# Moving left products behind the last head outputs, one exponential earlier, and a new order of one segment in four

## The chip, the cores and the metric

The kernel runs on one core of one Trainium2 chip. The metric is the device time of a whole execution in microseconds (us), from the slowest core, which here is the only one. Five engines take part: PE (TensorE, the matrix products), DVE (VectorE), ACT (ScalarE), POOL (GpSimd) and SP (SyncE, which here issues nearly all transfers). Each engine works through its own instructions in the order in which they were written, and waits on semaphores for the others. Sums of products stand in PSUM, eight banks of 2 KB for each of 128 partitions; all else that is in use stands in SBUF, and the program calls it the arena.

## The reference, cut to what matters

A recurrent attention with memory tokens (A), a gated feed-forward network (B), and a mix of both by a gate per row.

```python
for s in range(64):                                # 2048 positions, 32 to a segment
    h = concatenate([mem, x[:, 32*s:32*s+32]])     # 8 memory rows and 32 positions, 640 wide
    q, k, v = h @ Wq, h @ Wk, h @ Wv               # 32 heads of 192
    p = softmax(where(mask, (q @ k.T) * scale, -1e9))
    o = (p @ v) @ Wo                               # summed over the heads
    mem = o[:, :8]; outs.append(o[:, 8:])
a = concatenate(outs)
b = (gelu(x @ w_gate) * (x @ w_up)) @ w_down       # 640 -> 1536 -> 640
out = g * a + (1 - g) * b                          # g = sigmoid((x * gate_w).sum(-1))
```

The memory rows of a segment come out of the segment before it, so that the 64 segments are worked one after the other, and each ends with a chain on which the next one waits.

## The kernel before, in words

The feed-forward part comes first (the first 180 us or so) and leaves its result in DRAM. The rest of the time are the 64 segments, 22 to 24 us each.

**Octets, groups and steps.** The 32 heads of a segment are four octets of eight heads, which the text numbers in the order of work: first to fourth octet, `i` = 0 to 3 in the code (odd segments take them in reverse order, so that the weights loaded last are used first). Queries, keys and values of the octets are made in six groups (`GROUPS`, L523): Q and K of the first octet; V of the first with Q and K of the second; V of the second with Q and K of the third; V of the third with Q of the fourth; K of the fourth; V of the fourth. A group is accumulated in five projection steps, each over 128 of the 640 input columns, an item `("g", n, k)` for step `k` of group `n` (`proj`, L1110). A step of one product is four matmuls side by side, in the four column strips of TensorE (L1132; where the stationary operand is kept from the product before, L226). After the fifth step ScalarE copies the result out of PSUM (queries and keys L1153, values L1156).

**One octet behind its projections.** Each of these is an item in the list of the segment:

- `("tq", i)`, `("tk", i)`: VectorE transposes the rows of queries and keys (L1170); GpSimd copies a part of the queries (L1173).
- `("sc", i)`: scores (`scores`, L1177): the mask as a product (L1181), then the products of queries and keys (L1189, L234, L1196); VectorE takes the maximum (L1208) and subtracts it (L1210).
- `("ex", i)`: softmax (L1213): the exponential on ScalarE (L1220), the sum (L1222), its reciprocal (L1224) and the division (L1226, L1227) on VectorE.
- `("pt", i)`: the probabilities are transposed on TensorE (L1243, L1248) and copied out by ScalarE (L1261; for the fourth octet L1255, with VectorE at L1257).
- `("pv", i)`: head outputs, values times probabilities (`pv_oct`, L1264; products L1276 and L1278), copied out by ScalarE (L1308, for the fourth octet L1298) and VectorE (L1302).
- `("wo", i, h)`: output products, half `h` of octet `i`: two products by two slices ("pairs") of the output weights. L1326 for the first three octets, L1352 for the last four pairs; at place 3 (below) L1370.

The head outputs ask for a free bank of PSUM (`misc_bank`, L1100), as each group does at its first step: the bank that has been free for longest.

**Places.** A place is the number of a segment modulo four. Of the 40 rows of a segment, 32 go through the projections of the segment itself: the 8 memory rows and 24 positions. The queries, keys and values of its last 8 positions don't depend on the segment before, and those of four segments, 32 rows, are made together ahead of time: these are the *left products* (`left_mm`, L911; product L924, and L226 with the kept operand). The item `("lf", place, u, k)` is step `k` (0 to 4) of unit `u`, two product steps (queries and keys) for the next group of four segments; `("le", place, u, m)` copies them out (L1397 on). All places but place 3 walk the same list, but an `lf` or `le` item is executed only in segments of its place, and only where there is a later group of segments (15 of the 16 segments of each place). Place 0 has one unit, place 1 two, place 2 one. At place 3 the list is another: the output products are made for its own rows and for the left rows of the whole group together (`wo_both`, L1366), and `("vb", k)` are left products of values. `PROGS` (L546) names the list of each place, and `segment` (L1449) walks it. The order of the work on every engine is the order of these lists, written out by hand; semaphores follow from what each operation reads and writes.

**Weights.** The weights of the attention don't fit into SBUF. In each segment 13 pieces of the query, key and value weights (384 KB each) and 3 of the output weights (480 KB) are loaded again, in place of a piece just used: after each item, `swap_loads` (L644) issues on SP the transfer of the piece that comes into the slot of one that the item has used up (`load_piece`, L627), and the transfer waits for the last product that reads the old piece. What is loaded is needed late in the same segment: by the fourth octet's projections and the last output products.

**The end of a segment.** The last output products (L1352) are added up with the earlier ones by VectorE (L1567) and transposed (L1570); the first projection steps of the next segment that use the memory rows wait for that.

The stretch of the list around the change, for places 0 to 2 (L524 on):

```python
("ex", 2), ("lf", 2, 1, 2), ("pv", 1), ("wo", 0, 0), ("g", 4, 0), ...
("g", 5, 0), ("g", 5, 1), ("lf", 1, 1, 2), ("lf", 0, 1, 1), ("pt", 2), ("wo", 0, 1), ("tk", 3), ("sc", 3),
("pv", 2), ("g", 5, 2), ("wo", 1, 0), ("ex", 3), ("g", 5, 3), ("wo", 1, 1), ("g", 5, 4), ("wo", 2, 0),
("pt", 3), ("lf", 0, 1, 2), ("wo", 2, 1), ("pv", 3), ("wo", 3, 0), ("wo", 3, 1), ...
```

and the walk over it:

```python
for n, item in enumerate(PROGS[q]):
    ...
    elif kind == "lf":
        if i == q and unit(s, item[2]):
            ...
            left_mm(*unit(s, item[2]), item[3], unit_piece)
    ...
    swap_loads(s, item)
```

Of the kernel before, what the change touches and what calls it, by code (L numbers as in the profile page):

```python
# [238 lines left out]
def _build(nc, A_x, A_mem0, A_Wq, A_Wk, A_Wv, A_Wo, seg_len, w_gate, w_up, w_down,  # L239
# [278 lines left out]
    def piece_view(key, o):  # L518
        if key[0] == 3:
# [4 lines left out]
    PROG = [("g", 0, 0), ("g", 0, 1), ("g", 0, 2), ("g", 0, 3), ("g", 0, 4), ("tq", 0), ("g", 1, 0), ("g", 1, 1),  # L524
# [12 lines left out]
    PROG3 = [("g", 0, 0), ("g", 0, 1), ("g", 0, 2), ("g", 0, 3), ("g", 0, 4), ("g", 1, 0), ("tq", 0), ("tk", 0),  # L537
# [8 lines left out]
    PROGS = (PROG, PROG, PROG, PROG3)  # L546
    assert NOCT == 4
    WOP = 4
    NWP = NT
# [14 lines left out]
    def seg_order(s):  # L564
        keys = []
        for item in PROGS[s % 4]:
            if item[0] == "g":
# [810 lines left out]
    mids, n_wos, to_store = set(), [], []  # L1378
    for x, prog in enumerate(PROGS):
        at = prog.index  # L1380
# [5 lines left out]
        for u in range(2):  # L1386
# [6 lines left out]
            else:  # L1393
                assert at(("le", x, u, 0)) > max(at(("wo", 3, 1)), at(("pv", 3)))
    nqkvs = [[i for i, item in enumerate(prog) if item[0] == "g"][-1] for prog in PROGS]

# [36 lines left out]

    assert all(prog.index(("wo", NOCT - 2, 1)) < prog.index(("pv", NOCT - 1)) for prog in PROGS[:3])
    assert all(prog.index(("sc", NOCT - 1)) < prog.index(("pv", NOCT - 2)) and ("g", 3, EK) in prog[:prog.index(("sc", NOCT - 1))] for prog in PROGS)
    ek_at = [prog.index(("pv", NOCT - 2)) for prog in PROGS]

# [176 lines left out]
def bass_gated_mix__memory_aug_recurrent_mem_tr__glu_gated_geglu__prompt_kernel(  # L1614
    nc,
    A_x,
    A_mem0,
    A_Wq,
    A_Wk,
    A_Wv,  # L1620
    A_Wo,
    A_seg_len,
    B_x,
    B_w_gate,
    B_w_up,
    B_w_down,
    gate_w,
    out,
):
    _build(nc, A_x, A_mem0, A_Wq, A_Wk, A_Wv, A_Wo, A_seg_len, B_w_gate, B_w_up, B_w_down, gate_w, out)  # L1630
# [33 lines left out]
```

## Time and profile before

| | before |
|---|---|
| three runs | 1675.04, 1670.88, 1674.64 us |
| their median | 1674.64 us |
| the profiled execution | 1667.93 us |
| its span, first to last instruction | 1666.2 us |
| PE, products | busy 1567.0 us, 94%, 37090 instructions |
| PEld, weight loads of TensorE (beside PE) | 773.4 us, 46% |
| DVE | 998.3 us, 60% |
| ACT | 783.7 us, 47% |
| POOL | 546.0 us, 33% |
| granted TensorE clock | 0.995 of full speed |
| transfers | 499.28 MB, 300 GB/s on average; the queue of the weights holds the 16 DMA engines for 84.3% of the span |

The profile is one execution, recorded instruction by instruction. Three views of it are used. One gives, for a list of stretches of time, each engine's busy time in the stretch: from left to right the stretch and its length, the busy time and number of instructions of PE, PEld, DVE, ACT and POOL, the granted clock, the busy share of the DMA engines, and GB/s. The second is a time line: start, duration in us, engine, line, operation, destination and source, the tile with its type, and the number of instructions that the row joins; brackets at the end hold the time waited ahead of it and the operation that ended the wait. Several matmuls are in flight together, so that a row of products is counted from its start to the start of the row behind it. The third lists, for one line, what ended its waits: engine and line, us in total, how often. The rows of transfers ("DMA issues") give the engine that issues, how many, KB of each and the median us from issue to landing.

### The profile page before, as it was taken

The numbers are of one execution on the slowest core, as the hardware profiler recorded it, in microseconds if no ns is written. First come the engines' busy times: TensorE is split into PE (matmuls) and PEld (weight loads), VectorE is DVE, ScalarE is ACT, GpSimd is POOL, SyncE is SP. The second block draws the span as 40 slices with busy tenths as digits, with TensorE's granted clock in tenths as the row PEclk, the third lists the DMA queues.
The fourth block names the chain that finished last, engine by engine and source line by source line (L and its number), as shares of the span: only waits on it lengthen the run. The fifth ranks groups of instructions, "written<-read, shape, count | busy, mean of one in ns | idle before, by whom it ended". The sixth has DMA issues, their size and how long they took to land. (4 is left out here: it accounts for less than half of the span.)

```text
span 1666.2 us, 75811 instructions
## 1 busy us (share of the span) xinstructions
PE 1567.0 (94%) x37090; PEld 773.4 (46%) x28147; DVE 998.3 (60%) x3023; ACT 783.7 (47%) x1874; POOL 546.0 (33%) x1609
## 2 busy tenths in 40 slices
PE   9999899999999999999999999999999999999986
PEld 4444345444444445454444444454544444444543
DVE  6453566666566666666665666656665656656653
ACT  2222454545455454545454554545454555545452
POOL 1110233333333333333333333333333333333332
PEclk9999999999999999999999999999999999999998
DMA  9915999989899898989888898989888888988894
GB/s 292 345 47 157 321 319 324 317 315 313 310 323 334 299 323 292 331 317 332 299 310 302 317 343 283 313 290 326 322 296 309 301 326 318 316 292 311 312 326 163
DMA packets 275415, 499.28 MB, mean 300 GB/s; under 512 B 121119, under 2 KB 136327, under 8 KB 275079
## 3 DMA queue, kind: packets, MB, share of 16 engines
q1 hardware_dynamic: 271000, 491.30, 84.3%
q8 instruction: 255, 4.18, 1.0%
q10 hardware_dynamic: 4079, 3.14, 0.6%
q14 instruction: 81, 0.66, 0.1%
HBM read 473.25 MB, written 21.09 MB: 297 GB/s over the span
## 5 line engine op out<-in xcount | busy, mean ns | idle before, releaser
L1132 PE MATMUL ps<-arena 128*32 128x384 bf16 x8640 | 640.3, 329 | 19.6 <-DVE arena L1570 11.4
L226 PE MATMUL ps<-arena 128*32 128x384 bf16 x8960 | 635.9, 327 | 3.5 <-ACT arena L1153 1.2
L1132 PEld LDWEIGHTS ps<-arena 128*32 128x32 bf16 x8640 | 226.8, 96 | 390.8 <-issue 270.0
L1170 DVE STREAM_TRANSPOSE arena<-arena 128x384 bf16<-128x384 bf16 x512 | 273.7, 559 | 71.5 <-ACT arena L1153 70.2
L1153 ACT ACTIVATE arena<-ps 128x384 bf16<-128x384 f32 x512 | 230.3, 493 | 109.7 <-PE ps L1132 102.0
L1173 POOL COPY arena<-arena 64x160 bf16<-64x160 bf16 x256 | 81.3, 318 | 371.0 <-DVE arena L1170 368.9
L1326 PE MATMUL ps<-arena 128*32 128x320 bf16 x3456 | 180.9, 300 | 5.7 <-issue 3.2
L1156 ACT ACTIVATE arena<-ps 128x384 bf16<-128x384 f32 x256 | 124.9, 488 | 112.4 <-PE ps L1132 112.4
L1208 DVE TENSOR_REDUCE arena<-ps 104x4 f32<-104x160 f32 x256 | 83.0, 324 | 149.9 <-PE ps L1196 149.9
L1308 ACT ACTIVATE arena<-ps 128x480 bf16<-128x480 f32 (+1 forms) x208 | 116.6, 561 | 102.7 <-PE ps L1278 99.4
L1261 ACT ACTIVATE arena<-ps 128x448 bf16<-128x448 f32 x192 | 104.6, 545 | 122.8 <-PE ps L1248 122.6
L1006 POOL COPY arena<-arena 128x96 bf16<-128x96 bf16 x256 | 69.4, 271 | 231.1 <-PE ps L1196 159.4
L1222 DVE TENSOR_REDUCE arena<-ps 104x4 f32<-104x160 f32 x256 | 82.5, 322 | 97.6 <-ACT ps L1220 96.7
L1220 ACT ACTIVATE ps<-ps 104x160 f32<-104x160 f32 x256 | 75.7, 296 | 136.8 <-DVE ps L1210 134.9
L1370 PE MATMUL ps<-arena 128*64 128x320 bf16 x1536 | 124.9, 305 | 1.4 <-issue 0.6
L1276 PE MATMUL ps<-arena 128*64 128x160 bf16 x1536 | 119.0, 241 | 3.6 <-issue 3.5
L1326 PEld LDWEIGHTS ps<-arena 128*32 128x32 bf16 x3456 | 90.8, 96 | 47.2 <-ACT arena L1255 11.2
L924 PE MATMUL ps<-arena 128*32 128x384 bf16 x1280 | 108.7, 328 | 0.7 <-issue 0.7
L1278 PE MATMUL ps<-arena 128*64 128x64 bf16 x1536 | 104.3, 193 | 2.4 <-issue 2.1
L1316 POOL COPY arena<-arena 128x96 bf16<-128x96 bf16 x192 | 51.3, 267 | 162.7 <-ACT arena L1298 97.0
L1276 PEld LDWEIGHTS ps<-arena 128*64 128x64 bf16 x1536 | 81.7, 109 | 48.3 <-ACT arena L1156 19.4
L1398 ACT ACTIVATE arena<-ps 128x384 bf16<-128x384 f32 x120 | 57.2, 490 | 92.5 <-DVE arena L1570 41.4
(102 smaller groups left out, 2351.7 us busy)
## 6 DMA issues: line engine op xcount, KB each, us to landing
arena<-in_A_Wk_dram SPq DMA_DIRECT2D x335, 384.0 KB, 6.4
arena<-in_A_Wv_dram SPq DMA_DIRECT2D x335, 384.0 KB, 8.7
arena<-in_A_Wo_dram SPq DMA_DIRECT2D x205, 480.0 KB, 5.9
arena<-in_A_Wq_dram SPq DMA_DIRECT2D x209, 384.0 KB, 5.6
arena<-left_qk_scratch SPq DMA_DIRECT2D x126, 96.0 KB
left_qk_scratch<-arena SPq DMA_DIRECT2D x49, 192.0 KB, 5.2
left_qk_scratch<-arena SPq DMA_DIRECT2D x30, 96.0 KB, 5.5
ffn_b_scratch<-arena ACTq DMA_DIRECT2D x16, 160.0 KB, 4.1
```

The costliest lines, as they stand in the source:

```text
L226: return e.add_instruction(mybir.InstMatmult(name=nm, start_tensor_calc=like["start"], stop_tensor_calc=stop, tile_size=(128, 32), tile_po ...
L924: fns.append(lambda e, outp=outp, rhs=rhs, j=j: e.matmul(outp, lhs, rhs, start=(k == 0), stop=(k == KT - 1), tile_position=(0, 32 * j)))
L1132: fns.append(lambda e, outp=outp, rhs=rhs, j=j: e.matmul(outp, lhs, rhs, start=(k == 0), stop=(k == KT - 1), tile_position=(0, 32 * j)))
L1153: S_.add("act", lambda e, m=m, bk=bk: e.activation(out=rows_sb[m], in_=ps[:, bk, 0:384], func=ACTF.Copy), reads=[r_ps[bk]], writes=[r_rows ...
L1156: S_.add("act", lambda e, i=i, bk=bk: e.activation(out=v_sb[i % NVB].rearrange("p (c n) -> p c n", c=3), in_=ps[:, bk, 0:384].rearrange("p ...
L1170: S_.add("dve", lambda e: e.transpose(out=dst[:, :, 0:L], in_=rows_sb[m].rearrange("p (c r) -> p c r", r=L)), reads=[r_rows[m]], writes=[r ...
L1261: S_.add("act", lambda e: e.activation(out=PT, in_=ps[:, bank, 0:PTW + 128], func=ACTF.Copy), reads=[r_ps[bank]], writes=[r_PT], name="pT ...
L1276: return [lambda e: e.matmul(full, v[:, e0:e0 + 64], PTm[:, i], start=True, stop=False, tile_position=(0, 64 * i), skip_group_check=True), ...
L1278: lambda e: e.matmul(part, vl[:, e0:e0 + 64], PTl[:, i], start=False, stop=True, tile_position=(0, 64 * i), skip_group_check=True)]
L1308: S_.add("act", lambda e: e.activation(out=apx(u[:, 0, 0, :], [[rs, na], [3 * rs, 4], [1, R]]), in_=ps[:, A, 0:na * W].rearrange("p (c t r ...
L1326: fns.append(lambda e, i=i, t=t, j=j, gv=gv: e.matmul(ps[32 * j:32 * j + 32, bank, 0:2 * DJ].rearrange("p (h n) -> p h n", h=2), lhs2[i], ...
L1370: S_.add("pe", [lambda e, i=i, g_=g_, c=c, p=p: e.matmul(ps[64 * i:64 * i + 64, LB, 0:2 * DJ], U3[:, p % 4, c, :], g_[:, c, 2 * DJ * i:2 * ...
```

## The change

Three edits, all to the written-out orders.

1. **Places 0 to 2**, list `PROG`. Item `("lf", 2, 1, 2)`, a left product step of place 2, goes from between `("ex", 2)` and `("pv", 1)` to behind `("pv", 3)`, the fourth octet's head outputs. Items `("lf", 0, 1, 1)`, ahead of `("pt", 2)`, and `("lf", 0, 1, 2)`, between `("pt", 3)` and `("wo", 2, 1)`, both of place 0, go there too. All stand ahead of `("wo", 3, 0)`, the first of the last output products.
2. **Place 1** gets a list of its own, `PROG1`: `PROG` with `("ex", 3)`, the fourth octet's softmax, ahead of `("pv", 2)` instead of two items behind it.
3. **Place 3**, list `PROG3`, is written in another order. The projection steps keep their order among themselves, the output products and the left value products theirs, and so do the loads behind each kind. The fourth octet's key steps `("g", 4, 2)` and `("g", 4, 3)` now stand ahead of the output products `("wo", 0, 0)`, and its last value step `("g", 5, 4)` ahead of `("wo", 2, 0)`; the second scores follow the first step of group 3, with the first head outputs right behind them, which stood three steps later; transpositions and softmaxes move by some places.

The group numbered 4 holds the keys of the fourth octet and group 5 its values. Nothing is added to or taken from the work: each segment executes the same items as before.

```diff
--- before.py
+++ after.py
@@ -526,24 +526,26 @@
             ("g", 2, 2), ("lf", 1, 0, 0), ("pt", 0), ("tq", 1), ("tk", 1), ("sc", 1), ("g", 2, 3), ("g", 2, 4),
             ("tq", 2), ("ex", 1), ("lf", 2, 1, 0), ("lf", 1, 0, 1), ("lf", 1, 0, 2), ("pv", 0), ("g", 3, 0),
             ("tk", 2), ("g", 3, 1), ("g", 3, 2), ("g", 3, 3), ("pt", 1), ("lf", 2, 1, 1), ("g", 3, 4), ("sc", 2),
-            ("ex", 2), ("lf", 2, 1, 2), ("pv", 1), ("wo", 0, 0), ("g", 4, 0), ("g", 4, 1), ("lf", 0, 1, 0),
-            ("g", 4, 2), ("lf", 1, 0, 3), ("lf", 1, 0, 4), ("lf", 1, 1, 0), ("lf", 1, 1, 1), ("le", 1, 0, 0),
-            ("tq", 3), ("g", 4, 3), ("le", 1, 0, 1), ("g", 4, 4), ("g", 5, 0), ("g", 5, 1), ("lf", 1, 1, 2),
-            ("lf", 0, 1, 1), ("pt", 2), ("wo", 0, 1), ("tk", 3), ("sc", 3), ("pv", 2), ("g", 5, 2), ("wo", 1, 0),
-            ("ex", 3), ("g", 5, 3), ("wo", 1, 1), ("g", 5, 4), ("wo", 2, 0), ("pt", 3), ("lf", 0, 1, 2),
-            ("wo", 2, 1), ("pv", 3), ("wo", 3, 0), ("wo", 3, 1), ("lf", 2, 1, 3), ("lf", 2, 1, 4), ("le", 2, 1, 0),
-            ("le", 2, 1, 1), ("lf", 1, 1, 3), ("lf", 1, 1, 4), ("le", 1, 1, 0), ("le", 1, 1, 1), ("lf", 0, 1, 3),
-            ("lf", 0, 1, 4), ("le", 0, 1, 0), ("le", 0, 1, 1)]
-    PROG3 = [("g", 0, 0), ("g", 0, 1), ("g", 0, 2), ("g", 0, 3), ("g", 0, 4), ("g", 1, 0), ("tq", 0), ("tk", 0),
-            ("g", 1, 1), ("g", 1, 2), ("sc", 0), ("g", 1, 3), ("ex", 0), ("g", 1, 4), ("tq", 1), ("g", 2, 0),
-            ("tk", 1), ("g", 2, 1), ("g", 2, 2), ("g", 2, 3), ("g", 2, 4), ("sc", 1), ("tk", 2), ("g", 3, 0),
-            ("pt", 0), ("tq", 2), ("g", 3, 1), ("g", 3, 2), ("g", 3, 3), ("ex", 1), ("pv", 0), ("g", 3, 4),
-            ("sc", 2), ("pt", 1), ("ex", 2), ("g", 4, 0), ("g", 4, 1), ("wo", 0, 0), ("g", 4, 2), ("g", 4, 3),
-            ("g", 4, 4), ("tq", 3), ("tk", 3), ("wo", 0, 1), ("pv", 1), ("sc", 3), ("g", 5, 0), ("pt", 2),
-            ("wo", 1, 0), ("wo", 1, 1), ("ex", 3), ("pv", 2), ("g", 5, 1), ("g", 5, 2), ("g", 5, 3), ("pt", 3),
-            ("wo", 2, 0), ("g", 5, 4), ("wo", 2, 1), ("pv", 3), ("vb", 0), ("vb", 1), ("vb", 2), ("wo", 3, 0),
+            ("ex", 2), ("pv", 1), ("wo", 0, 0), ("g", 4, 0), ("g", 4, 1), ("lf", 0, 1, 0), ("g", 4, 2),
+            ("lf", 1, 0, 3), ("lf", 1, 0, 4), ("lf", 1, 1, 0), ("lf", 1, 1, 1), ("le", 1, 0, 0), ("tq", 3),
+            ("g", 4, 3), ("le", 1, 0, 1), ("g", 4, 4), ("g", 5, 0), ("g", 5, 1), ("lf", 1, 1, 2), ("pt", 2),
+            ("wo", 0, 1), ("tk", 3), ("sc", 3), ("pv", 2), ("g", 5, 2), ("wo", 1, 0), ("ex", 3), ("g", 5, 3),
+            ("wo", 1, 1), ("g", 5, 4), ("wo", 2, 0), ("pt", 3), ("wo", 2, 1), ("pv", 3), ("lf", 2, 1, 2),
+            ("lf", 0, 1, 1), ("lf", 0, 1, 2), ("wo", 3, 0), ("wo", 3, 1), ("lf", 2, 1, 3), ("lf", 2, 1, 4),
+            ("le", 2, 1, 0), ("le", 2, 1, 1), ("lf", 1, 1, 3), ("lf", 1, 1, 4), ("le", 1, 1, 0), ("le", 1, 1, 1),
+            ("lf", 0, 1, 3), ("lf", 0, 1, 4), ("le", 0, 1, 0), ("le", 0, 1, 1)]
+    PROG3 = [("g", 0, 0), ("g", 0, 1), ("g", 0, 2), ("g", 0, 3), ("g", 0, 4), ("tq", 0), ("g", 1, 0), ("tk", 0),
+            ("g", 1, 1), ("g", 1, 2), ("g", 1, 3), ("sc", 0), ("ex", 0), ("g", 1, 4), ("g", 2, 0), ("g", 2, 1),
+            ("g", 2, 2), ("g", 2, 3), ("pt", 0), ("tq", 1), ("tk", 1), ("g", 2, 4), ("g", 3, 0), ("sc", 1),
+            ("pv", 0), ("g", 3, 1), ("tq", 2), ("tk", 2), ("g", 3, 2), ("g", 3, 3), ("ex", 1), ("g", 3, 4),
+            ("sc", 2), ("g", 4, 0), ("g", 4, 1), ("g", 4, 2), ("g", 4, 3), ("pt", 1), ("tq", 3), ("wo", 0, 0),
+            ("ex", 2), ("g", 4, 4), ("wo", 0, 1), ("tk", 3), ("pv", 1), ("g", 5, 0), ("pt", 2), ("sc", 3),
+            ("wo", 1, 0), ("ex", 3), ("wo", 1, 1), ("pv", 2), ("g", 5, 1), ("g", 5, 2), ("g", 5, 3), ("pt", 3),
+            ("g", 5, 4), ("wo", 2, 0), ("wo", 2, 1), ("pv", 3), ("vb", 0), ("vb", 1), ("vb", 2), ("wo", 3, 0),
             ("wo", 3, 1), ("vb", 3), ("vb", 4)]
-    PROGS = (PROG, PROG, PROG, PROG3)
+    PROG1 = [item for item in PROG if item != ("ex", 3)]
+    PROG1.insert(PROG1.index(("pv", 2)), ("ex", 3))
+    PROGS = (PROG, PROG1, PROG, PROG3)
     assert NOCT == 4
     WOP = 4
     NWP = NT
```

## The prediction

> **What bounds the kernel now.** I read the page's first lines, then the busy time of each engine in four neighbouring segments (places 0, 1, 2, 3 in that order of rows), then what TensorE waited for at the line of the last output products (L1352).
>
> ```profile
> span 1666.2 us, 75811 instructions
> ```
>
> ```profile
> 1374.66:1397.76 23.10, 22.01 (x613) 11.34 (x473) 15.56 (x49) 10.65 (x28) 7.89 (x24) 1.00 0.86 303
> 1306.03:1328.76 22.73, 21.70 (x593) 10.26 (x433) 14.69 (x47) 12.39 (x31) 7.64 (x24) 1.00 0.92 321
> 1328.76:1350.63 21.87, 20.66 (x553) 9.68 (x412) 13.81 (x45) 11.54 (x29) 7.88 (x25) 1.00 0.94 333
> 1350.63:1374.66 24.03, 23.13 (x508) 12.04 (x389) 13.22 (x43) 11.84 (x29) 9.80 (x27) 1.00 0.83 300
> ```
>
> ```profile
>   DVE arena L1302: 14.6, 34
>   ACT arena L1298: 6.8, 14
>   DMA arena<-in_A_Wo_dram: 5.6, 12
> ```
>
> The first number behind the comma is TensorE's busy time: 20.7 to 23.1 us of each segment, and the granted clock (third from the right) is 1.00. So TensorE's own stream sets the time, and only its holes can be won: some 1.1 us in each of these segments. The largest regular hole is in the last three rows: at places 0 to 2 the last output products wait for the copies of the fourth head output out of PSUM (34 + 14 = 48 times, once in each such segment, 21.4 us together, 0.45 us each). The second bound is the transfers: at place 2 the DMA engines are at 0.94 of their time.
>
> **Prices.** All from place 2, segment 50, on TensorE, and then VectorE's row for the key transposition of the fourth octet there.
>
> ```profile
> 1340.29 0.26 PE L1189 MATMUL ps<-arena 128*40 128x40 bf16 x8
> ...
> 1341.02 0.26 PE L1276 MATMUL ps<-arena 128*64 128x160 bf16 x2
> ...
> 1341.44 0.59 PE L1326 MATMUL ps<-arena 128*32 128x320 bf16 x12
> 1341.85 1.31 PE L1132 MATMUL ps<-arena 128*32 128x384 bf16 x28
> 1342.99 0.21 PE L1243 MATMUL ps<-arena 104*32 104x80 bf16 x4
> ...
> 1349.53 0.39 PE L1352 MATMUL ps<-arena 128*32 128x160 bf16 x12 [0.25 <-DMA arena<-in_A_Wo_dram]
> ```
>
> ```profile
> 1343.41 0.58 DVE L1170 STREAM_TRANSPOSE arena<-arena 128x384 bf16<-128x384 bf16 x1 [0.24 <-ACT arena L1153]
> ```
>
> Seven product steps take 1342.99 - 1341.85 = 1.14 us, 0.163 us each. A left item is two such steps, 0.325 us. Head outputs take 1341.44 - 1341.02 = 0.42 us until the next kind of product.
>
> **Place 0 (15 segments; the last group has no left products).** Rows of segment 52: TensorE, then VectorE's two transpositions of the fourth octet; then, from place 2, the weight load of the last output product ahead of the fourth head outputs.
>
> ```profile
> 1390.50 0.26 PE L1189 MATMUL ps<-arena 128*40 128x40 bf16 x8
> ...
> 1394.37 0.26 PE L1276 MATMUL ps<-arena 128*64 128x160 bf16 x2
> ...
> 1395.35 0.80 PE L1352 MATMUL ps<-arena 128*32 128x160 bf16 x33 [0.49 <-ACT arena L1298]
> ```
>
> ```profile
> 1389.10 1.06 DVE L1170 STREAM_TRANSPOSE arena<-arena 128x384 bf16<-128x384 bf16 x2
> ```
>
> ```profile
> 1347.31 0.09 PEld L1326 LDWEIGHTS ps<-arena 128*32 128x32 bf16 x1 [0.35 <-ACT arena L1255]
> ```
>
> Two items move. The first, from ahead of the third octet's probability transposition, lets all behind it come 0.325 us earlier; next late is the key transposition, done at 1390.16, 0.34 before the scores at 1390.50. With 0.06 us from its end to the start of the scores, 0.28 is won. The second stood between the fourth octet's transposition and its head outputs. There place 2, which has no item, waits 0.35 us for ScalarE's copy (L1255), as long as the item lasts: taking it away wins 0 (bounds 0 and 0.33). Both then run behind the head outputs: 1394.37 + 0.42 + 4 x 0.163 = 1395.44, against 1395.35 now, 0.09 later, the 0.49 us of waiting being filled. Net 0.28 - 0.09 = 0.19, in a few segments less because other stalls stand there: 0.17 x 15 = **2.6 us won** (bounds 0 and 7). No queue is passed: these items issue no DMA.
>
> **Place 2 (15 segments).** The item between the third octet's scores and the second head outputs goes, and with it two changes of tile shape: scores to head outputs took 1341.02 - 1340.29 = 0.73 us, and will take about 0.23. But the key transposition of the fourth octet, for which the scores then wait, can start only 0.24 us sooner, VectorE being busy before that. So 0.24 us arrive at the fourth head outputs, and behind them 0.325 us of item go into the 0.45 us hole at no cost. Then stands the last piece of the output weights. Of the 12 waits for it on the list above eight are at place 2, the last the row at 1349.53, the first this one:
>
> ```profile
> 338.76 0.39 PE L1352 MATMUL ps<-arena 128*32 128x160 bf16 x12 [0.52 <-DMA arena<-in_A_Wo_dram]
> ```
>
> ```profile
> arena<-in_A_Wo_dram SPq DMA_DIRECT2D x205, 480.0 KB, 5.9
> ```
>
> A piece of 480 KB at the 333 GB/s of that segment takes 1.5 us, yet lands 5.9 us after its issue: it stands in a queue of some 4 us. Issued 0.24 us sooner it waits 0.24 us longer. So eight of 15 segments win nothing, and the others up to 0.24: 7 x 0.15 = **1.0 us won** (bounds 0 and 15 x 0.24 = 3.6). The page "DMA: Bandwidth & Descriptors" of the Trainium skill says, under "Queues, rings and completion order", that each DMA engine takes descriptors of a ring in order, which speaks against this part of the change; the same page says under "Two DMAs through the same engine are not ordered" that only the starts are in order. By the first rule place 2 wins the 1.0 us, by free completion it could win the 3.6; the 5.9 us of the row agree with the first.
>
> **Place 1 (16 segments).** Rows of segment 49: ScalarE's copy of the third head outputs and the exponential; VectorE's subtraction; TensorE's output products of the third octet and the transposition behind them.
>
> ```profile
> 1322.80 0.57 ACT L1308 ACTIVATE arena<-ps 128x480 bf16<-128x480 f32 x1 [0.84 <-PE ps L1278]
> 1323.27 0.30 ACT L1220 ACTIVATE ps<-ps 104x160 f32<-104x160 f32 x1
> ```
>
> ```profile
> 1322.85 0.33 DVE L1210 TENSOR_TENSOR ps<-ps,arena 104x160 f32<-104x160 f32 x1
> ```
>
> ```profile
> 1324.00 0.58 PE L1326 MATMUL ps<-arena 128*32 128x320 bf16 x12
> 1324.59 0.21 PE L1243 MATMUL ps<-arena 104*32 104x80 bf16 x2
> ```
>
> The swap on ScalarE adds a wait: the copy now stands behind an exponential that waits for the subtraction, done at 1323.18. The exponential comes at most 0.09 us sooner; the copy ends at about 1323.18 + 0.30 + 0.57 = 1324.05 instead of 1323.37, and the output products that read it start at 1324.00. They come up to 0.1 late, into the slack of 0.18 ahead of the transposition (twelve products take 0.41, so 1324.41 against 1324.59). Taken: 0.05 x 16 = **0.8 us won** (bounds 1.4 won, 1.6 lost).
>
> **Place 3 (16 segments).** Rows of segment 51: TensorE at the end of the segment, TensorE at the end of the third group of products, and ScalarE's copies of that group.
>
> ```profile
> 1368.46 1.01 PE L1370 MATMUL ps<-arena 128*64 128x320 bf16 x12
> 1369.39 0.35 PE L1132 MATMUL ps<-arena 128*32 128x384 bf16 x4
> 1369.67 1.01 PE L1370 MATMUL ps<-arena 128*64 128x320 bf16 x12
> 1370.51 0.24 PE L1276 MATMUL ps<-arena 128*64 128x160 bf16 x2
> ```
>
> ```profile
> 1357.40 0.50 PE L226 MATMUL ps<-arena 128*32 128x384 bf16 x8
> ```
>
> ```profile
> 1357.63 0.49 ACT L1156 ACTIVATE arena<-ps 128x384 bf16<-128x384 f32 x1 [1.05 <-PE ps L1132]
> 1358.02 0.87 ACT L1153 ACTIVATE arena<-ps 128x384 bf16<-128x384 f32 x2
> ```
>
> Twelve output products take 1370.51 - 1369.67 = 0.84 us; ahead of a projection step they take 0.93, and the step until the next ones 0.28 instead of 0.163. A change of tile shape costs 0.09 one way and 0.12 back, 0.21 a pair. The new order has two pairs fewer: second scores and first head outputs stand together, and the last value step stands ahead of both output items. That wins 0.42. It is paid back in part: the first head outputs write the PSUM bank of the third octet's queries (the oldest free one by the bank rule), and in the old order they came four steps after its copy. Now they follow the end of that group (1357.40 + 0.325 = 1357.73) by two steps, a change and the scores: 0.325 + 0.12 + 0.08 + 0.23 = 0.75 us. The copy ends at 1358.02 + 0.49 = 1358.51, and about 0.27 later in the new order, because the probabilities' copy has moved ahead of it on ScalarE: 1.05 after the group's end, 1.1 with the step to TensorE. A new wait of about 0.35. Queued behind it is all of TensorE's stream. Net 0.42 - 0.35 = 0.07, and some 0.03 of smaller waits: 0.1 x 16 = **1.6 us won** (bounds 6.7 won without the wait, and 4.5 lost if it is twice as long).
>
> **The sum.** 2.6 + 1.0 + 0.8 + 1.6 = 6.0 us. The profiled execution took 1667.9 us (span 1666.2), below the median of the three timed runs, 1674.6 us; carried over to that median: **1668.6 us**, 0.36% faster. Differences under 0.3% (5 us) can't be told from no change.
>
> **Rivals.** (1) A transfer takes the place of the wait, and the kernel is slower. At place 3 the third and fourth key steps of the fourth octet now stand ahead of the output products (0.84 us and a change of shape, 0.93 us sooner). If their pieces land less than 0.93 us before their present use, TensorE waits in every such segment: 16 x 0.93 = 14.9 lost, 1668.6 + 14.9 = 1683.5; the sum turns at 6.0 / 16 = 0.38 us a segment. Against it: 300 GB/s at this place, so that pieces of 393 KB land 1.3 us apart, and the fifth step, used 0.16 us behind the fourth, waits rarely; where it doesn't wait, the fourth piece is there 1.1 us early. Chance 0.18. (2) Nothing measurable: place 0 wins nothing because the key transposition or another copy is as late, and place 3's wait eats all. 1.8 us are left: 1672.8. Chance 0.27. (3) The change does more: place 3's wait is hidden behind ScalarE's queue and place 2's piece comes sooner: 2.6 + 3.6 + 0.8 + 6.7 = 13.7, 1660.9. Chance 0.1. The forecast has 0.45.
>
> Range 1661 to 1680: from (3) to most of (1). Faster by over 0.3%: two thirds of the forecast's chance, all of (3), some of (2): 0.43. Slower: 0.18 with a little of (2): 0.2. The same: 0.37.
>
> **What would show it.** Right: at places 0 and 2 the waits of L1352 for L1302 and L1298 vanish, at place 1 they stay at 0.45; the waits of L1352 for the output weights grow at place 2; two fewer alternations of L1370 and L1132 at place 3, and a wait for ACT L1153 ahead of its first L1276. Wrong: place 2 shorter by 0.2 us in every segment, new waits of L1132 for the key weights at place 3, or no wait ahead of its first head outputs.

## The result, and the profile after

Over 20 runs of each, the changed kernel took 1663.51 us in the median and the kernel before 1669.72 us: a ratio of 0.9966, 95% interval [0.9951, 0.9981]. One of the changed kernel's 20 runs was slow (1750.02 us) and is left out of the ratio. By the ratio that is 5.7 us less (3.2 to 8.2; the medians differ by 6.2), where 6.0 were forecast. A second series of 12 runs gave 0.9948 [0.9931, 0.9965], 8.7 us.

The profiled execution after is one of the slower ones (1669.2 us, above its kernel's median; the one before, 1667.9 us, lay below its own). So its span proves nothing about the change:

```profile
span 1667.5 us, 75813 instructions
```

What can be read is the inside of the segments. The same four neighbouring segments of the profile after, in the order of places 1, 2, 3, 0, with the columns as before:

```profile
1308.71:1331.14 22.43, 21.38 (x592) 10.00 (x432) 14.66 (x47) 12.33 (x31) 7.93 (x24) 1.00 0.93 328
1331.14:1352.70 21.56, 20.90 (x556) 9.64 (x412) 13.69 (x45) 11.64 (x29) 7.79 (x24) 1.00 0.95 337
1352.70:1375.86 23.16, 22.31 (x508) 12.06 (x389) 13.10 (x43) 11.85 (x29) 9.66 (x27) 1.00 0.85 310
1375.86:1399.35 23.49, 22.48 (x614) 11.69 (x474) 15.71 (x49) 10.83 (x28) 8.00 (x24) 1.00 0.87 298
```

All but the last are shorter, but neighbours differ by more than that, so single segments don't decide. Better is the sum over all stretches of a place that the change touches. The next two fences are the sum rows of the stretches view, before and after, each for place 0 (from the fourth octet's first value step to the next segment, 14 segments), place 1 (from the fourth octet's scores, 16), place 2 (from the third octet's scores, 16) and place 3 (the whole segment, 15). The first number is the time, the others are the engines' busy time in it.

```profile
sum 126.23, PE 111.38 PEld 71.64 DVE 72.16 ACT 52.03 POOL 55.33; mean PE 7.96 PEld 5.12 DVE 5.15 ACT 3.72 POOL 3.95
sum 107.09, PE 91.57 PEld 57.06 DVE 54.80 ACT 43.44 POOL 53.21; mean PE 5.72 PEld 3.57 DVE 3.43 ACT 2.71 POOL 3.33
sum 170.20, PE 150.56 PEld 92.62 DVE 96.48 ACT 82.94 POOL 73.84; mean PE 9.41 PEld 5.79 DVE 6.03 ACT 5.18 POOL 4.61
sum 355.56, PE 343.10 PEld 179.86 DVE 197.14 ACT 178.23 POOL 141.93; mean PE 22.87 PEld 11.99 DVE 13.14 ACT 11.88 POOL 9.46
```

```profile
sum 121.23, PE 113.02 PEld 72.66 DVE 70.52 ACT 52.16 POOL 55.40; mean PE 8.07 PEld 5.19 DVE 5.04 ACT 3.73 POOL 3.96
sum 109.25, PE 91.47 PEld 58.15 DVE 55.60 ACT 43.26 POOL 53.80; mean PE 5.72 PEld 3.63 DVE 3.48 ACT 2.70 POOL 3.36
sum 173.69, PE 155.21 PEld 91.06 DVE 95.46 ACT 83.91 POOL 73.87; mean PE 9.70 PEld 5.69 DVE 5.97 ACT 5.24 POOL 4.62
sum 352.57, PE 337.08 PEld 182.29 DVE 197.75 ACT 178.43 POOL 143.48; mean PE 22.47 PEld 12.15 DVE 13.18 ACT 11.90 POOL 9.57
```

Places 0 and 3 are shorter (5.0 and 3.0 us), places 1 and 2 longer (2.2 and 3.5 us). The second trace of the same kernel has 123.46, 104.73, 174.95 and 353.80: place 1 alone moved by 4.5 us between two executions of one program, so its sum tells nothing; place 2 is longer both times than in the one trace of before.

The waits of the last output products, after (L1354 is the L1352 of before; all lines from here on are two higher, and in the fences of some later runs up to five, by their own edits). The two copies are L1304 and L1300:

```profile
  DMA arena<-in_A_Wo_dram: 6.9, 15
  DVE arena L1304: 6.0, 14
  issue: 3.2, 5
  ACT arena L1300: 2.0, 4
```

The waits for the copies went from 48 (21.4 us) to 18 (8.0 us): the 16 at place 1, and the two in the last group of segments, which has no left products. So the hole is filled at places 0 and 2, as forecast. What TensorE waits for instead, first before, then after; the columns are the total, how often, and the longest:

```profile
PE ps L1132 <- DMA arena<-in_A_Wv_dram: 2.3, 5, 0.7
PE ps L1132 <- DMA arena<-in_A_Wk_dram: 1.4, 2, 0.9
```

```profile
PE ps L1134 <- DMA arena<-in_A_Wv_dram: 8.8, 23, 0.7
PE ps L1278 <- ACT arena L1155: 3.4, 15, 0.2
PE ps L1134 <- DMA arena<-in_A_Wk_dram: 2.7, 2, 1.8
```

The second row of the last fence is the forecast new wait at place 3. The first was not forecast: the projection steps now wait 23 times for value weights, 19 of them at place 2 (2 of the 5 before). And one forecast sign is missing: at place 2 the last output products wait for their weights 8 times as before, 3.3 us before and 2.9 after (10 times and 3.5 us in the second trace). The rise of that line's total from 5.6 to 6.9 us is at places 0 and 1.

### The profile page after: what moved, and what is told of

It reads as the page before. It is cut to its first block, busy times and chain, and to the rows that moved or that the text cites. A ratio compares the mean times of both kernels' runs of the same rounds, so it can differ in the third digit from the quotient of the medians.

```text
span 1667.5 us, 75813 instructions
## 1 busy us (share of the span) xinstructions
PE 1566.5 (94%) x37107; PEld 779.2 (47%) x28147; DVE 1000.1 (60%) x3023; ACT 785.5 (47%) x1874; POOL 549.9 (33%) x1609
## 4 chain that ended last, share of the span: by engine, by line
PE 71%; DMA 17%; DVE 6%; ACT 3%; issue 3%; SPq 1%; POOL 0%; DVEq 0%; ACTq 0%; POOLq 0%
PE ps L1134 19%; PE ps L226 17%; DMA arena<-in_A_Wv_dram 9%; PE ps L1372 7%; DMA arena<-in_A_Wo_dram 6%; PE ps L1328 5%; PE ps L1278 3%; PE ps L835 3%; PE ps L832 3%; PE ps L1354 2%; PE ps L1183 2%; PE ps L926 2%; PE ps L858 2%; PE ps L1191 1%; DMA arena<-in_A_Wk_dram 1%
## 5 line engine op out<-in xcount | busy, mean ns | idle before, releaser
L1134 PEld LDWEIGHTS ps<-arena 128*32 128x32 bf16 x8640 | 231.9, 96 | 399.2 <-issue 258.9
L1328 PE MATMUL ps<-arena 128*32 128x320 bf16 x3456 | 184.4, 300 | 16.2 <-issue 11.1
L1278 PE MATMUL ps<-arena 128*64 128x160 bf16 x1536 | 116.9, 240 | 5.6 <-ACT arena L1155 3.4
L1328 PEld LDWEIGHTS ps<-arena 128*32 128x32 bf16 x3456 | 89.6, 96 | 62.2 <-issue 19.1
L1278 PEld LDWEIGHTS ps<-arena 128*64 128x64 bf16 x1536 | 81.2, 109 | 37.6 <-ACT arena L1158 14.4
```

What stands on the lines that cost most here:

```text
L1134: fns.append(lambda e, outp=outp, rhs=rhs, j=j: e.matmul(outp, lhs, rhs, start=(k == 0), stop=(k == KT - 1), tile_position=(0, 32 * j)))
L1278: return [lambda e: e.matmul(full, v[:, e0:e0 + 64], PTm[:, i], start=True, stop=False, tile_position=(0, 64 * i), skip_group_check=True), ...
L1328: fns.append(lambda e, i=i, t=t, j=j, gv=gv: e.matmul(ps[32 * j:32 * j + 32, bank, 0:2 * DJ].rearrange("p (h n) -> p h n", h=2), lhs2[i], ...
```

## The experiments

Theory: the prediction's, place by place. Rival, formed from the first trace: place 3 carries the gain, and place 2 is bound by its transfers. Ratios are to the kernel before on the same chip.

**The changed kernel again** (no edit).

> The changed kernel once more, for a second trace. Both theories: 0.9966 of the time before, the place-3 segments at about 23.2 us (23.7 before), the wait of the first head outputs at place 3 for ScalarE's copy of the queries 0.2 us in 15 segments. They differ on place 2: by the prediction its segments are some 0.07 us shorter than before on average, and the 0.3 us by which they were longer in the first trace is chance (stalls without a releaser, one trace); by the rival (place 2 is bound by its transfers, so that TensorE sooner means only waiting more) they come out as long as before or longer again, with the value-weight waits ahead of the projection steps at 8 to 9 us in total against 2.3 before.

Measured: 0.9948 [0.9931, 0.9965]; L1278 waits 3.4 us in 15 segments again, the projection steps 8.6 us (21 times) for value weights, place 2 at 174.95. One trace of before is too little to call place 2 longer, but the traces of all runs together show that it is no shorter: nine with the item moved and all transfers take 171.7 to 176.4 us, three with the old order 170.2 to 173.6.

**Place 3 alone**: the list `PROG3` of the change, `PROGS = (PROG, PROG, PROG, PROG3)` with the old `PROG`.

> Only the new order at place 3, the other places as before. The prediction's split: 1.6 us of 6.0, ratio 0.9990. The rival, from the medians of the first trace (23.66 to 23.20 us, 0.46 in each of 15 segments): 7 us, ratio 0.9958, which would be all of the gain. The first trace's means (0.2 us) would give 3 us, 0.9981.

Measured: 0.9958 [0.9936, 0.9979], 7.0 us (3.5 to 10.7). Its place-3 stretches, and below those of the run after it, which has the old order there:

```profile
sum 354.49, PE 337.91 PEld 181.30 DVE 197.79 ACT 178.43 POOL 143.02; mean PE 22.53 PEld 12.09 DVE 13.19 ACT 11.90 POOL 9.53
```

```profile
sum 356.17, PE 343.44 PEld 180.02 DVE 196.94 ACT 178.78 POOL 142.37; mean PE 22.90 PEld 12.00 DVE 13.13 ACT 11.92 POOL 9.49
```

Two traces of the old order have 355.56 and 356.17, these three of the new one 354.49, 352.57 and 353.80. One trace is not enough here: the four later runs below that keep this order, this bank and all transfers have 350.4 to 356.2, so that the seven average 353.2 against 355.9, 0.18 us a segment. Steadier is the commonest single segment, one without another wait, first of the kernel before, then of the changed one:

```profile
978.85:1002.20 23.35, 22.73 (x509) 11.97 (x390) 13.12 (x43) 11.90 (x29) 9.48 (x27) 1.00 0.85 307
1169.03:1192.19 23.16, 22.31 (x511) 12.07 (x388) 13.10 (x43) 11.84 (x29) 9.51 (x26) 1.00 0.85 309
```

That is 0.19 us a segment, 3.0 us in 16. The clock says more, but its interval begins just above that.

**Places 0, 1 and 2 alone**: the other half of the change, the old `PROG3`.

> The new orders at places 0, 1 and 2, the old one at place 3. The prediction's split: 2.6 + 0.8 + 1.0 = 4.4 us, ratio 0.9974. The rival (place 3 carries it): 1.000, with place 2 not shorter and the waits of the last output products for VectorE's and ScalarE's copies gone all the same at places 0 and 2.

Measured: 0.9966 [0.9948, 0.9985], 5.7 us (2.5 to 8.7). Both halves win; the rival's "place 3 carries it" falls. 7.0 and 5.7 are more than the 5.7 and 8.7 of the whole change; with these intervals it stays open whether the gains of the halves overlap.

**Another PSUM bank for the first head outputs at place 3.**

```diff
-    def misc_bank(s, group=9):
+    def misc_bank(s, group=9, want=None):
...
-        b = min(ok, key=lambda b: misc[b])
+        b = want if want in ok else min(ok, key=lambda b: misc[b])
...
+            if i == 1:
+                v1_bank[0] = bk
...
-        A = misc_bank(s)
+        A = misc_bank(s, want=v1_bank[0] if s % 4 == 3 and o == 0 else None)
```

> The changed kernel, but at place 3 the first head outputs write the PSUM bank of the second octet's values, whose copy is the first of the three behind that group, instead of the bank of the third octet's queries, whose copy comes second. If the new wait of 0.2 to 0.3 us there is what the prediction took it for (the bank), it vanishes and the place-3 segments come out 0.2 to 0.29 us shorter than the changed kernel's 23.2: some 4 us, ratio 0.994 to before. Rival: the head outputs then wait for the probabilities' copy, or the later second head outputs and the piece behind them are late instead: no difference to the changed kernel, 0.9966.

Measured: 0.9946 [0.9922, 0.9971], not told from the changed kernel. The time line of TensorE in segment 51, second scores and first head outputs, changed kernel first:

```profile
1360.31 0.26 PE L1191 MATMUL ps<-arena 128*40 128x40 bf16 x8
...
1360.89 0.26 PE L1278 MATMUL ps<-arena 128*64 128x160 bf16 x2 [0.23 <-ACT arena L1155]
```

```profile
1353.78 0.26 PE L1194 MATMUL ps<-arena 128*40 128x40 bf16 x8
...
1353.98 0.26 PE L1281 MATMUL ps<-arena 128*64 128x160 bf16 x2
...
1357.57 0.35 PE L1134 MATMUL ps<-arena 128*32 128x384 bf16 x4 [0.63 <-DMA arena<-in_A_Wk_dram]
```

From scores to head outputs 0.58 us became 0.20: the wait was the bank's, and it cost 0.38 us. (The bracket shows only 0.23, because idle time is counted from the end of the last score product, and products overlap.) And the last row shows where the 0.38 went in this segment: the fourth octet's fourth key step now waits for its weights. Such waits stand in 9 of the 15 segments here, 4.8 us in all; the two traces of the changed kernel have 2 (2.7 us) and 7 (6.0 us), so the total alone proves little. But the segments say the same: the whole 0.38 arrives at the end of one only (22.77 us against 23.16), and the sum of the 15 is 351.82 us, where without this edit it was 353.2 on average.

**Place 2's left item back at its old place.**

```diff
+    PROG2 = [item for item in PROG if item != ("lf", 2, 1, 2)]
+    PROG2.insert(PROG2.index(("pv", 1)), ("lf", 2, 1, 2))
-    PROGS = (PROG, PROG1, PROG, PROG3)
+    PROGS = (PROG, PROG1, PROG2, PROG3)
```

> The changed kernel with place 2's left item back between the third octet's softmax and the second head outputs. The prediction: 1.0 us of the gain goes (7 of 15 segments by 0.15), ratio some 0.0006 nearer to 1 than the changed kernel's. The rival (place 2 is bound by its transfers): the time of the changed kernel; place 2's segments from the third octet's scores on take as long as with the item moved (10.9 us, before 10.7), the waits of the projection steps for value weights fall from 8.7 to about 3 us in total, and the waits of the last output products for VectorE's and ScalarE's copies at place 2 come back (0.45 us each, 7 us).

Measured: 0.9980 [0.9959, 1.0001], some 2 to 5 us slower than the changed kernel, by intervals that touch. In the trace the rival is right: the waits for value weights fall to 2.4 us (7 times), those for the copies rise to 11.2 + 3.4 = 14.6 us, and place 2's stretches take 173.56 us, against 173.69 and 174.95 with the item moved. One wait takes the other's place. The clock's 2 to 5 us don't appear in place 2's stretches; whether they are real stays open.

**Relief for place 2**: two of its 16 transfers left out, so that the products there use the weights that stood there before.

```diff
             if other is None or (other in partner) == (seg % 2 == 0):
                 continue
+            if seg % 4 == 2 and other[0] == 0:
+                loaded[slot_id[other]] = other
+                continue
             load_piece(other, "swap s%d" % seg)
```

> The changed kernel without the transfers of the two reloaded query pieces in place-2 segments (two of 16 pieces, 0.79 MB; those segments multiply by the weights that stood there before, so the output is another). If place 2 is bound by its transfers, its segments get shorter by the 0.65 us or so that the projections and the last output products wait for weights there (22.4 to about 21.7 us, 10 us in all). If its transfers are only late now and then: 22.4 to 22.2 at most, 3 us.

**The same with the item at its old place.**

> The same without those two transfers, with place 2's left item back at its old place. Beside the run before it this measures what the moved item is worth when the weights are there in time. The prediction's walk on TensorE: 0.24 us a segment longer than with the item moved, 3.6 us in 15 segments. If the third octet's scores and the fourth's key transposition don't bound it there, up to 0.5 us a segment, 7.5 us. If the moved item is worth nothing even then, the two runs are alike.

Measured: 0.9873 [0.9842, 0.9904] with the item moved, 0.9935 [0.9909, 0.9960] with the item at its old place. The stretches of place 2, item moved and item back:

```profile
sum 159.14, PE 152.18 PEld 92.68 DVE 94.70 ACT 84.12 POOL 73.97; mean PE 9.51 PEld 5.79 DVE 5.92 ACT 5.26 POOL 4.62
```

```profile
sum 166.29, PE 149.85 PEld 92.30 DVE 96.51 ACT 83.17 POOL 73.46; mean PE 9.37 PEld 5.77 DVE 6.03 ACT 5.20 POOL 4.59
```

With fewer bytes the changed kernel's place 2 falls from 173.69 to 159.14, 0.9 us a segment: it is bound by its transfers. And where the weights are there in time, the moved item is worth 166.29 - 159.14 = 7.2 us in these two traces; the ratios of the two kernels differ by 0.0062, some 10 us. How the transfers take that back is seen on TensorE's time line in a place-2 segment: the changed kernel (segment 46, one of its longest), from the first output products over the fourth octet's key steps to its first two value steps, and then the end of the segment; below, the same steps with two pieces less (segment 46 again).

```profile
1251.25 1.31 PE L1134 MATMUL ps<-arena 128*32 128x384 bf16 x19
1253.20 0.50 PE L1134 MATMUL ps<-arena 128*32 128x384 bf16 x5 [0.64 <-DMA arena<-in_A_Wv_dram]
1254.19 0.35 PE L1134 MATMUL ps<-arena 128*32 128x384 bf16 x4 [0.49 <-DMA arena<-in_A_Wv_dram]
...
1260.96 0.39 PE L1354 MATMUL ps<-arena 128*32 128x160 bf16 x12 [0.38 <-DMA arena<-in_A_Wo_dram]
```

```profile
1239.61 1.31 PE L1137 MATMUL ps<-arena 128*32 128x384 bf16 x28
```

Seven steps that take 1.14 us in one run of 28 products are broken up by two waits of 1.1 us together (the steps take 2.0 us longer, so the brackets hold only a part of it), and a third one stands ahead of the last output products. So the pieces for the value steps are the first to be late, seven us ahead of the piece that the prediction named.

**The key steps behind the output products again**, on top of the other bank.

```diff
+    moved = [("g", 4, 2), ("g", 4, 3)]
+    PROG3 = [item for item in PROG3 if item not in moved]
+    at4 = PROG3.index(("g", 4, 4))
+    PROG3[at4:at4] = moved
```

> The changed kernel with the other PSUM bank for the first head outputs at place 3 and, besides, the fourth octet's third and fourth key steps back behind the first output products, where they stood before the change. In the run with the other bank alone the wait for the copy went (0.38 us sooner at the first head outputs), but the key steps then waited 0.5 us a segment for their weights. If that is the whole reason, this costs one more pair of changes of tile shape (0.21) and saves 0.5: place-3 segments of 23.45 on average go to about 23.15, 4 to 5 us below the run with the bank alone, ratio 0.992. Rival: the transfers only move their wait to the fifth key step or the last value steps: 23.4, ratio 0.9946.

Measured: 0.9949 [0.9925, 0.9974]. The waits for key weights fall from 4.8 us to 0.6 us (once), and place 3's stretches from 351.82 to 349.93 us, 0.13 a segment instead of the expected 0.3. At the same time the last output products wait 10.7 us (21 times) for their weights, 4.9 (14 times) with the bank alone. The clock sees no gain. But neither theory is shown by that. 0.13 us is within what one trace differs from another, and key-weight waits lay between 1.1 and 6.0 us in the seven traces of the new order without this edit. And the added waits for output weights are none of place 3's: they stand at places 0 to 2 (4.6, 1.8 and 4.3 us), and in the last run below, which has the same two edits, they come to 4.1 us (11 times). So that the transfers took the gain back here is not shown.

**Place 0's second item back.**

```diff
+    PROG0 = [item for item in PROG if item != ("lf", 0, 1, 2)]
+    PROG0.insert(PROG0.index(("pt", 3)) + 1, ("lf", 0, 1, 2))
```

> The changed kernel with the second of place 0's two items back between the fourth octet's probability transposition and its head outputs. The prediction said that its removal wins nothing (ScalarE's copy of the probabilities is as late) and that behind the head outputs both items together outlast the hole by 0.09 us. So at place 0 the head outputs come at the same time as in the changed kernel, and the last output products 0.1 us sooner or, by what the copy is late, the same: 0 to 1.4 us in all, not to be told by the clock. Rival: the item did delay the head outputs, which then come up to 0.33 us later, 5 us in all.

Measured: 0.9974 [0.9952, 0.9996]. Place 0's stretches take 122.27 us, between the 121.23 and 123.46 of the two traces of the changed kernel. So the second item is worth nothing to be seen, and by subtraction the first one carries what place 0 wins.

**Place 1's softmax back**: `PROGS = (PROG, PROG, PROG, PROG3)`.

> The changed kernel with the fourth octet's softmax at place 1 back behind the third head outputs. The prediction: 0.05 us a segment, 0.8 us in all, not to be told by the clock; ScalarE's copy of the third head outputs comes 0.6 us sooner and the exponential at most 0.1 us later. Rival: the earlier exponential is what made the third group of output products and all behind it come sooner at place 1 (0.1 to 0.2 us in the traces), and the kernel gets 1.6 to 3.2 us slower.

Measured: 0.9958 [0.9934, 0.9981]; place 1's stretches 107.67 us, between 109.25 and 104.73. The swap makes no difference that these runs can show.

**Place 1's hole filled.**

```diff
+    for item, nxt in ((("tq", 3), ("le", 1, 0, 0)), (("lf", 1, 1, 2), ("wo", 3, 0))):
+        PROG1.remove(item)
+        PROG1.insert(PROG1.index(nxt), item)
```

> The changed kernel with place 1's hole filled too: its left item ahead of the third probability transposition goes behind the fourth head outputs, and the fourth octet's query transposition goes ahead of the copying out of the first unit there, so that the scores of the fourth octet don't wait for GpSimd's part of the queries. On TensorE alone 0.3 us a segment are to be had, 4.8 us. If the transfers bound place 1 as they do place 2, the last piece of the output weights, which lands within 0.15 us of its use in 5 to 7 of 14 segments, eats half or more: 2 us or less, and its waits at place 1 grow to nearly every segment.

Measured: 0.9960 [0.9938, 0.9982]. The waits for the copies fall to 1.4 us (3 times), so the hole is filled, and place 1's stretches take 106.40 us: inside the spread again. What eats the gain there is a wait that the changed kernel does not have, all of it at place 1: the fourth octet's scores, which now come sooner, wait for VectorE's key transposition.

```profile
PE ps L1194 <- DVE arena L1175: 2.4, 12, 0.2
```

The wait of the scores' mask for GpSimd's copy, which the earlier query transposition was to avoid, stands once at place 1 in both kernels (0.3 us); the others, 13 in the changed kernel and 18 here, are at place 2.

**All three together**: the other bank, the key steps, place 1 filled.

> All that looked better in the traces together: the other PSUM bank at place 3 with the key steps behind the output products (0.2 us a segment, 3.2 us), and place 1 filled (0 to 4.8 us). If TensorE's walk counts, 1664 - 3 - 5 = 1656 us, ratio 0.990. If the transfers take it back, no better than the changed kernel: 0.995.

Measured: 1658.7 us, 0.9927 [0.9898, 0.9955], 12 us below the kernel before. It has the lowest ratio of all these kernels that do the whole work, between the two expectations; each of the two parts alone (0.9949, 0.9960) was no better than the changed kernel, and the interval still touches the changed kernel's, so that it stays open why they do more together.

## Why the prediction was right, step by step

**The time**: 1668.6 us was forecast, 6.0 below the median then known; 5.7 and 8.7 were measured. That the sum fits so well is in part luck: place 2's 1.0 us is not there, place 1's 0.8 us cannot be seen, and place 3 won about twice its 1.6. With the figures below, 2.6 us at place 0 and 3.0 at place 3 make 5.6. The median itself came out 5.1 us lower than forecast, because the three runs of before that it was carried over to lay 4.9 us above the later median of 20.

**Place 0** (2.6 us): right in mechanism. The rows of segment 52 after, VectorE's key transposition, then TensorE's scores, fourth head outputs, first left product and last output products:

```profile
1391.72 0.58 DVE L1172 STREAM_TRANSPOSE arena<-arena 128x384 bf16<-128x384 bf16 x1 [0.80 <-ACT arena L1155]
```

```profile
1392.35 0.28 PE L1191 MATMUL ps<-arena 128*40 128x40 bf16 x8
...
1396.30 0.26 PE L1278 MATMUL ps<-arena 128*64 128x160 bf16 x2
...
1396.72 0.35 PE L926 MATMUL ps<-arena 128*32 128x384 bf16 x4
...
1397.38 0.84 PE L1354 MATMUL ps<-arena 128*32 128x160 bf16 x36
```

The transposition ends at 1392.30 and the scores start 0.05 us later: it is what is late next, as the working said. From the fourth head outputs to the last output products it is 1.08 us instead of 0.98, the forecast 0.09 and no wait. The sums of the traces (126.2 and 126.4 with the old order, 120.7 to 124.8 in ten traces with the first item moved and all transfers) give 3.7 us in 14 segments. The stalls of the last section are in them: without the waits listed as "issue" it is 2.4 us, 0.17 a segment (2.6 us in 15), as forecast. That the second item wins nothing was shown by itself.

**Place 2** (1.0 us): right that the transfers take back what TensorE wins, wrong about which of them. The step that failed: "So 0.24 us arrive at the fourth head outputs ... Then stands the last piece of the output weights." In between lie five value steps, and the weights of some had been just in time: in the trace before, the second step's piece landed 0.18 us (median of 16 segments) ahead of its use, in the changed kernel TensorE mostly stands waiting for it. There the 0.5 us won at the second head outputs is already stopped. Nothing is won that the traces show (170.2 to 173.6 us with the old order, 171.7 to 176.4 with the item moved). What the move is worth with two pieces less is 7.2 / 15 = 0.48 us a segment, twice the 0.24 of the walk; in that pair of runs the last output products of place 2 also wait less for their weights, 0.2 us against 3.7, and without these 3.5 us it is 0.24 a segment, the walk's figure.

**Place 1** (0.8 us): too small to be shown either way, as its bounds said.

**Place 3** (1.6 us): right in mechanism, small in size: 0.1 a segment was forecast, 0.19 is seen. The new wait is there in 15 segments and costs 0.38 us, 0.35 was forecast; other bank, no wait. The sign "two fewer alternations of L1370 and L1132" is miscounted: by the prediction's own working, and in the traces, one of the two pairs is between scores and head outputs. What was left out is that the key steps may then wait a little more for their weights (1.4 and 1.0 us in two traces of the old order, 1.1 to 6.0 in seven of the new one).

**Rival 1** (key weights at place 3, 14.9 us lost) is refuted in its size: at most 5 us. Its working put the pieces 1.3 us apart; neighbours of 384 KB landed 0.98 us apart (median of the trace before). Its mechanism is real, and it eats a part of the next gain: take the bank's wait away, and the key steps wait in 9 of 15 segments. That the change's own new wait of 0.38 us covered the transfers in part follows from that, but was not tried by itself. **Rival 2** (nothing measurable) is excluded by both intervals, **rival 3** (13.7 us) by both too: the part of it that counted on place 2's piece coming sooner is what the transfers refuse.

On the rule of the Trainium skill ("DMA: Bandwidth & Descriptors", "Queues, rings and completion order") that a ring is worked in order: the trace after agrees with it. Of the 1020 weight pieces whose landing it holds, none landed ahead of one that was issued earlier, and the 3.6 us that free completion could have given place 2 did not come. The relief runs, in which the waits for value weights (8.8 us) vanished from the list, don't tell the two rules apart: two pieces less bring the later ones forward under either.

## What to carry to other kernels

Before a hole on the busiest engine is filled, look how long ahead of its use each transfer behind it lands: an engine that runs earlier reaches its weights earlier, and the first piece with less slack than the gain takes the rest; here that was not the piece that was waited for before. A wait that a new order adds can be priced from PSUM banks and copies as well as from data, and another bank is a cheap test of it. And where one profiled execution varies by more than the change, compare the stretch that the change touches, summed over all segments of a kind, in several traces.

## What the runs showed of the hardware

TensorE stalls that no other engine ends ("issue") take 21 to 27 us in each of the traces. After:

```profile
PE ps L1328 <- issue: 11.1, 17, 1.5
PE ps L1354 <- issue: 3.2, 5, 1.4
PE ps L1134 <- issue: 2.6, 6, 0.9
PE ps L1278 <- issue: 2.2, 4, 0.9
```

They stand at other lines in other kernels, which looks like chance. But counting the matmuls and weight loads of the trace up to each of the 30 stalls of over 0.25 us, the distances between neighbours are 256, 2046, 1792, 768, 4352, 1022, 2816 and so on: all are multiples of 256 to within 2. In the trace before, the distances of the 31 stalls begin with 1790, 254, 5630, 3836, 1280: the same grid, to within 6. The instruction queue of the page fits:

```profile
q8 instruction: 255, 4.18, 1.0%
```

255 packets of 16 KB, and the 37107 + 28147 = 65254 matmuls and weight loads of TensorE in the trace after are 254.9 times 256. So TensorE's instructions are fetched in blocks of 256, and about one block in eight comes late, by 0.3 to 1.5 us. The Trainium skill ("Runtime: NRT & Kernel Launch", "Instruction fetch mechanics") gives the same block and says that its cost is "mostly hidden"; here it is 1.3% of the time, two and a half to four times what the change won. That the queue of weights, which holds the DMA engines for 84% of the span, is what delays the blocks was not tried.
